# Exponentials and squares placed ahead of the cast of h's high part on ScalarE, in ticks that hold output products

## The chip, the cores and the metric

One core of a Trainium2 chip runs the whole program. The time is device time in microseconds (us) of one execution. The engines are TensorE (PE for its matmuls, PEld for its weight loads), VectorE (DVE), ScalarE (ACT), GpSimd (POOL) and SyncE (SP, which issues the DMAs). Each engine works through its own instructions in the order in which they stand.

## The reference

Windowed attention (8 batches, 8 heads, 576 positions, 64 wide; the first four heads look back 32 positions, the other four 128 positions in steps of 4), then RMS normalisation and a gated feed-forward, 512 to 1536 and back, over 4608 tokens:

```python
scores = np.where(masks[None], scale * np.matmul(q, k.transpose(0, 1, 3, 2)), -1e9)
attn = np.exp(scores - np.max(scores, axis=-1, keepdims=True))
attn = attn / (np.sum(attn, axis=-1, keepdims=True) + 1e-09)
x = np.matmul(attn, v).transpose(0, 2, 1, 3).reshape(B * S, H * D)
xn = x / np.sqrt(np.mean(x * x, axis=-1, keepdims=True) + 1e-06) * rms_g
g = xn @ w_gate
silu = g * (1.0 / (1.0 + np.exp(-g)))
return (silu * (xn @ w_val) @ w_out).astype(np.float32)
```

## The kernel before

The 4608 tokens are 16 units (u = 0 to 15) of 288. A unit's feed-forward runs over 12 blocks j of 128 hidden columns, and each block has three parts, called ticks here: gate (the product g, with `gate`), value (the product v, with `val`), and output, where `proj` multiplies h of the block before into four accumulators. A unit has so 36 ticks. From unit 1 on every operand x, w and h is split into a high part (rounded to the matmul's short format) and a low part (the rest), and each product is three matmuls: high by high, high by low, low by high (`three`, L652 and L655).

While the feed-forward of unit u runs, the attention of unit u + 1 is spread over its ticks: 14 bursts (a pair of heads c, a block i of queries) per unit. A burst has scores s (L508, L511), then the maximum on VectorE (`scores_max`, L384), exponentials on ScalarE (`scores_exp`, L395), the sum's reciprocal and a scaling on GpSimd (`scores_norm`, L411), transposes t of the weights on TensorE (L486), a copy pt of them out of PSUM on ScalarE with its low part on VectorE (`untranspose`, L466 and L468), output products o (L495 or L499), and their copy into xraw (`take` on ScalarE, L428 or L431; from unit 3 on `add` on VectorE, L441, for the low parts). When the last block of a pair of heads has been taken, `square` makes its squares for the norm (L447).

Nothing of this order is left to a scheduler: it is written out by hand. What follows a matmul group is put off with `later(dt, rank, fn)`: it is issued dt ticks later, and at the start of each tick `flush` issues what is due, smallest rank first, equal ranks as they came. Then the tick's matmuls are issued. In an output tick the ranks that bear on the change are: the product h = silu(g) * v on VectorE (`prod`, L710, rank 0), the copy pt (0.2), the casts of h's high part on ScalarE (`parts`, L721, 0.5) with its low part on GpSimd (L722), the copies by `take` (0.5), the exponentials (2), the squares (2.5), casts of k and q (3, 3.1) and of v's high part (3.3).

For PSUM two banks, "g" and "v", alternate between gate and value products: v of block j + 1 uses the bank that held g of block j. Where transposes fall into the output tick of block j, they are written into that same bank, so the value product of block j + 1 may not begin before ScalarE (L466) and VectorE (L468) have read them. This happens, for attention units from 3 on, after the blocks j = 1, 3, 5 and 11.

The tiles named in the profile: g, v and acc are the PSUM tiles of the three products, th the tanh and then h, hhi and hlo its parts, t the scores, weights or (on TensorE) the transposed weights, sum the row maxima and sums, pt the transposed weights in SBUF, sq the squares, xraw the attention's output.

Of the kernel before, what the change touches and what calls it, by code (L numbers as in the profile page):

```python
# [29 lines left out]
NEX = 3  # L30
# [31 lines left out]
def geometry(u, c):  # L62


    half = u % 2
    if c < NC // 2:
        if half:
            return [(QB * i, QB * i, 0, P) for i in range(U // QB)], QB, U + W
        return [(QB * i, max(QB * i - W, 0), 0 if i else W, P if i else QB)
                for i in range(U // QB)], QB, U  # L70
    nq = U // DIL
    keys = nq + (W if half else 0)
    return [(nq * r, keys * r, 0 if half else W, keys) for r in range(DIL)], nq, keys * DIL
# [3 lines left out]
def attn_moe(ctx: ExitStack, tc: tile.TileContext, qk_in, v_in, w_gate, w_val, w_out, rms_g, outT):  # L77
# [38 lines left out]
    now = [0]  # L116
    put_off = {}

    def later(dt, rank, fn):
        put_off.setdefault(now[0] + dt, []).append((rank, fn))  # L120
# [182 lines left out]
    def further(b, n):  # L303

        k = everything.index(b) + n
        return everything[k] if k < len(everything) else None
# [83 lines left out]
    def scores_exp(u, c, i):  # L390
        blocks, nq, _ = geometry(u, c)
        n = blocks[i][3]
        t, sm = st[u, c, i]
        for a in range(2):
            A.activation(out=t[:nq, a, :n], in_=t[:nq, a, :n], func=AF.Exp, scale=-1.0,  # L395
                         bias=sm[:nq, a, 0:1], accum_out=sm[:nq, a, 1:2] if u or i % 2 else None)
# [18 lines left out]
    def take(u, c, i, o):  # L415

        blocks, nq, _ = geometry(u, c)
        if (u, c) not in xraw:
            xraw[u, c] = sb.tile([P, U], F32, tag="xraw", name=f"xraw_{u}_{c}", bufs=NC)
        x = xraw[u, c]  # L420
        if c < NC // 2:
            to = x[:, QB * i:QB * i + nq]
        else:
            to = x.rearrange("p (j r) -> p r j", r=DIL)[:, i, :]
        copy = V.tensor_copy if i % 2 and u == 0 and c == NC - 1 else A.copy
        if u < NEX:
            for a in range(2):
                copy(out=to[a * D:(a + 1) * D], in_=o[a * D:(a + 1) * D, a * nq:(a + 1) * nq])  # L428
        else:
            for a in range(2):  # L430
                A.copy(out=to[a * D:(a + 1) * D], in_=o[a * D:(a + 1) * D, (2 + a) * nq:(3 + a) * nq])  # L431
        if i == len(blocks) - 1:
            later(1 if c != 1 or u < NEX else 4, 2.5 if u else 1.9, lambda: square(u, c))

    def add(u, c, i, o):
        _, nq, _ = geometry(u, c)
        x = xraw[u, c]
        to = x[:, QB * i:QB * i + nq] if c < NC // 2 else x.rearrange("p (j r) -> p r j", r=DIL)[:, i, :]
        for a in range(2):
            rows = slice(a * D, (a + 1) * D)  # L440
            V.tensor_tensor(out=to[rows], in0=o[rows, a * nq:(a + 1) * nq], in1=to[rows], op=ALU.add)  # L441

    def square(u, c):
        first = c == 0
        sq = sb.tile([P, U], F32, tag="xsq" if first else "tmp", name=f"sq_{u}_{c}", bufs=1 if first else 2)
        x = xraw[u, c]
        A.activation(out=sq, in_=x, func=AF.Square)  # L447
        if u == 0:
            G.tensor_scalar(out=x, in0=x, scalar1=gs[:, c:c + 1], scalar2=1.0, op0=ALU.mult, op1=ALU.mult)
        if first:  # L450
            xsq[u] = sq
        else:
            later(1, 0.4, lambda: (V if c == NC - 1 or u == 1 else G).tensor_tensor(out=xsq[u], in0=xsq[u], in1=sq, op=ALU.add))
# [6 lines left out]
    def untranspose(b, t_ps, wait):  # L460
        blocks, nq, _ = geometry(*b[:2])
        n = blocks[b[2]][3]
        t_in = t_ps[:n].rearrange("k (a q) -> k a q", a=2)[:, :, :nq]
        exact = b[0] < NEX
        st[b] = pt = sb.tile([P, 2, 2, QB], F32 if exact else F32R, tag="pt", name=f"pt_{b[0]}_{b[1]}_{b[2]}", bufs=2)
        A.copy(out=pt[:n, 0, :, :nq], in_=t_in)  # L466
        def low_part():
            V.tensor_tensor(out=pt[:n, 1, :, :nq], in0=t_in, in1=pt[:n, 0, :, :nq], op=ALU.subtract)  # L468

        if not exact:  # L470
            later(1, 0.4 if wait > 1 else -1.5, low_part) if wait else low_part()

    def products(q, t, o, t_ps, s_tag="s", o_tag="o", wait=0):


        if q:
            s_ps = ps.tile([P, 512], F32, tag=s_tag, name=f"s_{q[0]}_{q[1]}_{q[2]}")
        if o:
            o_ps = ps.tile([P, 512], F32, tag=o_tag, name=f"o_{o[0]}_{o[1]}_{o[2]}")
            pt = st.pop(o)  # L480
        if t:
            p, _ = st.pop(t)
        def transposed(a):
            blocks, nq, _ = geometry(*t[:2])
            n = blocks[t[2]][3]
            PE.transpose(t_ps[:n, a * QB:a * QB + nq], p[:nq, a, :n], ident[:nq, :nq])  # L486

        def output(a):
            blocks, nq, _ = geometry(*o[:2])
            n = blocks[o[2]][3]  # L490
            if a:
                return
            out = o_ps[:, :2 * nq].rearrange("d (a q) -> d a q", a=2)
            if o[0] < NEX:
                PE.matmul(out, vs.pop(o)[:n].rearrange("k a d -> k (a d)"), pt[:n, 0, :, :nq], start=True, stop=True)  # L495
                return
            vh, vl = (part[:n].rearrange("k a d -> k (a d)") for part in vparts[everything.index(o) % 2])
            both = o_ps[:, :4 * nq].rearrange("d (t a q) -> d t a q", t=2, a=2)
            PE.matmul(both, vh, pt[:n, :, :, :nq], start=True, stop=False)  # L499
            PE.matmul(out, vl, pt[:n, 0, :, :nq], start=False, stop=True)  # L500

        def scored(a):
            blocks, nq, _ = geometry(*q[:2])
            qc, kc, _, n = blocks[q[2]]
            sv = s_ps[:QB].rearrange("q (a t k) -> q a t k", a=2, t=2)
            if q[0] < NEX:
                qk = heads[q[0], 2 * q[1] + a]
                PE.matmul(sv[:nq, a, 0, :n], qk[:, qc:qc + nq], qk[:, U + kc:U + kc + n], start=True, stop=True)  # L508
                return
            qs, ks = heads[q[0], 2 * q[1] + a]  # L510
            PE.matmul(sv[:nq, a, :, :n], qs[:, qc:qc + nq], ks[:, :, kc:kc + n], start=True, stop=True)  # L511

        order = ((t, transposed), (o, output), (q, scored))
        if t and t[0] >= NEX:
            order = ((o, output), (t, transposed), (q, scored))
        parts = [(b, fn, a) for b, fn in order for a in range(2)]
        for b, fn, a in parts:
            if b:
                fn(a)
        if t:  # L520
            later(1, 0.2, lambda: untranspose(t, t_ps, wait))
        if o:
            later(1, 0.5, lambda: take(*o, o_ps))
            if o[0] >= NEX:
                later(2, -0.3, lambda: add(*o, o_ps))
            if o[0] < NEX:
                later(1, 9, lambda: load_v(further(o, 3)))
            far = further(o, 2)
            if far and far[0] >= NEX:
                split_v(far, 8 if o[0] < NEX else 1)  # L530
        if q:
            later(1, 0.7, lambda: scores_max(*q, s_ps))
            later(2, 2, lambda: scores_exp(*q))
            later(3 if q[0] < NNAT else 4, -1, lambda: scores_norm(*q))
            u, c, i = q
            nxt = after(u, 2 * c, 2)
            nb = len(geometry(u, c)[0])
            if u < NEX:
                if u == NNAT - 1 and c == NC - 1 and i == nb - 1:
                    for h in range(4):  # L540
                        later(1, 9, lambda h=h: load(NNAT, h))
                if u >= NNAT and i == nb - 1 and c < NC - 1:
                    for a in range(2):
                        later(1, 9, lambda a=a: load(*after(u, 2 * c + a, 4)))
                if u == NEX - 1 and c == NC - 1 and i == nb - 1:
                    for a in range(2):
                        later(3 + a, 9, lambda a=a: split(NEX, a, (1, 2, 2, 3), G, G))
            elif nxt and i == 0:
                split(*nxt, (1, 2, 2, 3), G, G)
                split(nxt[0], nxt[1] + 1, (2, 3, 3, 4) if c < NC - 1 else (1, 2, 3, 4), G, G)  # L550
# [245 lines left out]
    ends = nb + LAG + OUT + 5  # L796
# [127 lines left out]
```

## Time and profile before

| | |
|---|---|
| median of 3 runs | 1130.6 us (1130.0 to 1130.92) |
| the profiled execution | 1130.35 us |
| its span from first to last instruction | 1128.3 us |
| granted TensorE clock | 1.000 |
| idle time of ScalarE ahead of h's high part (L721) | 180.2 us, in 115 of 180 |

The page of the profile has, for 40 equal slices of the span, the busy share of each engine in tenths:

```profile
PE   8999999999999999999999999999999999999998
PEld 5787999999999999999999999999999999999998
ACT  6794676656576665657656575665657657575311
```

A timeline row reads: start in us, duration in us, engine, source line, operation, tile written <- tiles read, shapes, count; in brackets the idle time of the engine just before it and the instruction that ended it. A row of waits reads: who waited <- for whom, us in total, how often, the longest. Spans of matmuls overlap, so the distance from one start to the next tells more than the duration.

### The profile page before, as it was taken

To read this page: it belongs to the slowest core of one execution; us is meant where nothing else is said; L and a number is where in the kernel's file an instruction comes from. 1 tells how busy PE (TensorE), PEld (TensorE's weight loads), DVE (VectorE), ACT (ScalarE), POOL (GpSimd) and SP (SyncE) were. 2 spreads that over 40 slices of the span, in tenths; PEclk is the share of its full clock that TensorE was granted. 3 is DMA by queue.
4 is the path that set the end of the run, shared out by engine and by line. 5 is a ranking of instruction groups with operands and counts; after the bars stand their busy time and mean duration, and the time that the engine had idled before them with its cause. 6 is when DMAs were issued, how large, how long until landed. Compare 5 with 4: busy or idle time off the path is not lost.

```text
span 1128.3 us, 25465 instructions
## 1 busy us (share of the span) xinstructions
PE 1114.0 (99%) x8362; PEld 1078.7 (96%) x8362; DVE 672.4 (60%) x2734; ACT 701.5 (62%) x2579; POOL 674.9 (60%) x1154
## 2 busy tenths in 40 slices
PE   8999999999999999999999999999999999999998
PEld 5787999999999999999999999999999999999998
DVE  7889667556565565656556565665656556565412
ACT  6794676656576665657656575665657657575311
POOL 7423578656586665757657575675657656584311
PEclk9999999999999999999999999999999999999999
DMA  9664212212131131312212121130312212120000
GB/s 258 185 245 178 75 52 83 75 34 80 42 91 50 41 93 32 94 39 63 73 39 83 41 84 51 46 95 27 88 42 78 62 34 78 46 78 15 6 17 22
DMA packets 61542, 82.16 MB, mean 73 GB/s; under 512 B 7298, under 2 KB 41090, under 8 KB 61410
## 3 DMA queue, kind: packets, MB, share of 16 engines
q1 hardware_dynamic: 61410, 80.54, 23.9%
q8 instruction: 66, 1.08, 0.4%
q14 instruction: 66, 0.54, 0.2%
HBM read 71.08 MB, written 9.44 MB: 71 GB/s over the span
## 4 chain that ended last, share of the span: by engine, by line
PE 80%; ACT 7%; DVE 7%; POOL 2%; issue 2%; DMA 1%; SPq 0%; DVEq 0%; ACTq 0%; POOLq 0%
PE v L655 14%; PE acc L655 14%; PE g L655 14%; PE v L652 8%; PE acc L652 7%; PE g L652 7%; PE s L511 2%; PE acc L649 2%; PE o L499 2%; PE v L649 2%; ACT t L395 2%; PE g L649 2%; PE t L486 1%; ACT pt L466 1%; DVE pt L468 1%
## 5 line engine op out<-in xcount | busy, mean ns | idle before, releaser
L722 POOL TENSOR_TENSOR hlo<-th,hhi 128x288 fp32r<-128x288 f32 x179 | 145.8, 814 | 178.6 <-ACT hhi L721 165.9
L655 PE MATMUL acc<-hhi,lo 128*128 128x288 f32 x720 | 212.6, 295 | 0.0
L697 DVE SCALAR_TENSOR_TENSOR th<-th,g 128x288 f32<-128x288 f32 x180 | 81.8, 454 | 209.0 <-ACT pt L466 134.7
L721 ACT CAST hhi<-th 128x288 fp32r<-128x288 f32 x180 | 78.0, 433 | 180.2 <-DVE th L710 180.2
L655 PE MATMUL g<-xhi,lo 128*128 128x288 f32 x612 | 180.3, 295 | 0.0
L655 PE MATMUL v<-xhi,lo 128*128 128x288 f32 x612 | 180.1, 294 | 0.0
L411 POOL TENSOR_SCALAR t<-t,sum 72x72 f32<-72x72 f32 (+3 forms) x414 | 151.6, 378 | 35.5 <-DVE sum L405 23.2
L395 ACT ACTIVATE t<-t,sum 96x128 f32<-96x128 f32 (+3 forms) x448 | 165.1, 372 | 7.2 <-DVE sum L384 6.7
L323 POOL TENSOR_TENSOR vlo<-vt,vhi 128x128 fp32r<-128x128 f32 x182 | 84.2, 463 | 136.5 <-ACT vhi L319 134.5
L692 ACT ACTIVATE th<-g 128x288 f32<-128x288 f32 x180 | 73.9, 411 | 126.3 <-PE g L486 71.7
L655 PEld LDWEIGHTS acc<-hhi,lo 128*128 128x128 f32 x720 | 135.4, 188 | 0.0
L441 DVE TENSOR_TENSOR xraw<-o,xraw 64x72 f32<-64x72 f32 (+1 forms) x364 | 97.1, 267 | 39.2 <-ACT xraw L431 36.6
L655 PEld LDWEIGHTS g<-xhi,lo 128*128 128x128 f32 x612 | 115.2, 188 | 0.0
L655 PEld LDWEIGHTS v<-xhi,lo 128*128 128x128 f32 x612 | 115.0, 188 | 0.0
L652 PE MATMUL acc<-hhi,hi_o 128*128 128x288 f32 x360 | 109.1, 303 | 0.0
L652 PE MATMUL g<-xhi,hi_g 128*128 128x288 f32 x357 | 106.9, 299 | 0.0
L655 PE MATMUL acc<-hlo,hi_o 128*128 128x288 f32 x360 | 106.4, 296 | 0.0
L710 DVE TENSOR_TENSOR th<-th,v 128x288 f32<-128x288 f32 x180 | 81.0, 450 | 38.4 <-PE v L655 32.5
L431 ACT COPY xraw<-o 64x72 f32<-64x72 f32 (+1 forms) x364 | 95.3, 262 | 9.7 <-PE o L500 7.6
L353 POOL TENSOR_TENSOR ks<-qk,ks 128x288 fp32r<-128x288 f32 (+2 forms) x104 | 93.3, 902 | 3.1
L655 PE MATMUL g<-xlo,hi_g 128*128 128x288 f32 x322 | 95.1, 295 | 0.0
L362 POOL TENSOR_TENSOR qs<-qk,qs 64x288 fp32r<-64x288 f32 x104 | 84.1, 809 | 15.3 <-ACT qs L357 8.6
(188 smaller groups left out, 3528.7 us busy)
## 6 DMA issues: line engine op xcount, KB each, us to landing
qk<-in_qk_dram SPq DMA_DIRECT2D x60, 288.0 KB, 2.8
vt<-in_v_dram SPq DMA_DIRECT2D x196, 64.0 KB, 1.9
qk<-in_qk_dram SPq DMA_DIRECT2D x30, 352.0 KB, 3.0
out_dram<-ot SPq DMA_DIRECT2D x64, 144.0 KB, 1.9
qk<-in_qk_dram SPq DMA_DIRECT2D x30, 304.0 KB, 2.9
raw<-in_w_gate_dram SPq DMA_DIRECT2D x12, 512.0 KB, 6.0
raw<-in_w_val_dram SPq DMA_DIRECT2D x12, 512.0 KB, 5.3
raw<-in_w_out_dram SPq DMA_DIRECT2D x12, 512.0 KB, 4.1
```

What stands on the lines that cost most here:

```text
L323: G.tensor_tensor(out=vl, in0=vs.pop(b), in1=vh, op=ALU.subtract)
L353: ek.tensor_tensor(out=ks[:, 1, :nkt], in0=kr, in1=ks[:, 0, :nkt], op=ALU.subtract)
L362: eq.tensor_tensor(out=qs[D:], in0=qr[D:], in1=qs[D:], op=ALU.subtract)
L395: A.activation(out=t[:nq, a, :n], in_=t[:nq, a, :n], func=AF.Exp, scale=-1.0, bias=sm[:nq, a, 0:1], accum_out=sm[:nq, a, 1:2] if u or i % ...
L411: (V if u == 0 and (c, i) > (NC - 1, 0) else G).tensor_scalar(out=t[:nq, a, :n], in0=t[:nq, a, :n], scalar1=sm[:nq, a, 3:4], scalar2=1.0, ...
L431: A.copy(out=to[a * D:(a + 1) * D], in_=o[a * D:(a + 1) * D, (2 + a) * nq:(3 + a) * nq])
L441: V.tensor_tensor(out=to[rows], in0=o[rows, a * nq:(a + 1) * nq], in1=to[rows], op=ALU.add)
L652: PE.matmul(out, wh[:, cc, :], xh, start=start, stop=False)
L655: PE.matmul(out, w[:, cc, :], v, start=False, stop=stop and k == 1)
L697: V.scalar_tensor_tensor(out=t, in0=t, scalar=1.0, in1=g, op0=ALU.add, op1=ALU.mult)
L710: V.tensor_tensor(out=t, in0=t, in1=v_ps[:, :U], op=ALU.mult)
L722: (V if (u, j) == (NU - 1, NJ - 1) else G).tensor_tensor(out=lo, in0=t, in1=hi, op=ALU.subtract)
```

## The change

Two ranks change. The exponentials of a burst whose scores were issued in a gate tick (`wait == 1`) come two ticks later, in an output tick; they get rank 0.42 in place of 2, and so stand behind pt (0.2) and ahead of h's high part (0.5) and of `take`. The squares of units from 3 on get 0.44 where they fall into an output tick.

```diff
         if i == len(blocks) - 1:
-            later(1 if c != 1 or u < NEX else 4, 2.5 if u else 1.9, lambda: square(u, c))
+            dt = 1 if c != 1 or u < NEX else 4
+            later(dt, 0.44 if u >= NEX and (now[0] + dt - ends) % 3 == 0 else 2.5 if u else 1.9, lambda: square(u, c))
...
             later(1, 0.7, lambda: scores_max(*q, s_ps))
-            later(2, 2, lambda: scores_exp(*q))
+            later(2, 0.42 if wait == 1 else 2, lambda: scores_exp(*q))
```

No instruction is added or removed, and only ScalarE's instructions change places: 77 pairs of exponentials and 26 squares. The diff lengthens the file by one line, so lines from 434 on have numbers one higher after it.

The first place is ScalarE's order in the output tick of block j = 1 in the feed-forward of unit 5, before the change (`hhi_1` and `th_1` are those of block 1; `t_2_1` is a burst of attention unit 6, `sq_0` its first squares, `pt_1_2` the copy that the next value product's bank waits for):

```order
L319 CAST vhi_2277<-vt_1_1_5446 128x128
L721 CAST hhi_1_5926<-th_1_5884 128x288
L395 ACTIVATE t_2_1_5891,sum_87<-t_2_1_5891,sum_87 72x72 x2
L447 ACTIVATE sq_0_5935<-xraw_0_5749 128x288
L466 CAST pt_1_2_5962<-t_1_5953 128x192
```

The same place in the changed kernel:

```order
L319 CAST vhi_2277<-vt_1_1_5446 128x128
L395 ACTIVATE t_2_1_5891,sum_87<-t_2_1_5891,sum_87 72x72 x2
L448 ACTIVATE sq_0_5928<-xraw_0_5749 128x288
L722 CAST hhi_1_5930<-th_1_5884 128x288
L467 CAST pt_1_2_5962<-t_1_5953 128x192
```

The two exponentials and the square now stand ahead of the cast, and the copy pt directly behind it.

The second place is the output ticks of blocks 3 and 4 of the same feed-forward and the two ticks between, on ScalarE, before:

```order
L721 CAST hhi_3_6121<-th_3_6081 128x288
L395 ACTIVATE t_3_0_6088,sum_90<-t_3_0_6088,sum_90 72x72 x2
L357 CAST qs_0_6127<-qk_0_5896 128x288
L466 CAST pt_2_2_6152<-t_3_6143 72x2x72
L431 COPY xraw_2_6155<-o_2_0_6145 64x72 x2
L357 CAST qs_1_6165<-qk_1_5931 128x288
L319 CAST vhi_2277<-vt_2_2_5974 128x128
L692 ACTIVATE th_4_6190<-g_4_6171 128x288
L395 ACTIVATE t_3_1_6158,sum_86<-t_3_1_6158,sum_86 72x72 x2
L466 CAST pt_2_3_6221<-t_4_6211 72x2x72
L721 CAST hhi_4_6223<-th_4_6190 128x288
L431 COPY xraw_2_6155<-o_2_1_6213 64x72 x2
```

And in the changed kernel:

```order
L395 ACTIVATE t_3_0_6088,sum_90<-t_3_0_6088,sum_90 72x72 x2
L722 CAST hhi_3_6123<-th_3_6081 128x288
L357 CAST qs_0_6127<-qk_0_5896 128x288
L467 CAST pt_2_2_6152<-t_3_6143 72x2x72
L431 COPY xraw_2_6155<-o_2_0_6145 64x72 x2
L357 CAST qs_1_6165<-qk_1_5935 128x288
L319 CAST vhi_2277<-vt_2_2_5974 128x128
L693 ACTIVATE th_4_6190<-g_4_6171 128x288
L395 ACTIVATE t_3_1_6158,sum_86<-t_3_1_6158,sum_86 72x72 x2
L467 CAST pt_2_3_6221<-t_4_6211 72x2x72
L448 ACTIVATE sq_1_6223<-xraw_1_5965 128x288
L722 CAST hhi_4_6225<-th_4_6190 128x288
```

After block 3 the exponentials of `t_3_0` have gone ahead of the cast; those of `t_3_1`, whose scores came in another tick, stay where they were. After block 4 the square `sq_1`, which stood behind the output copies (L431), has gone ahead of the cast and of these copies.

## The prediction

> **What bounds the kernel now.** I read the page first, then the waits grouped by who waited for whom, then the timeline around one such wait, engine by engine.
>
> ```profile
> span 1128.3 us, 25465 instructions
> PE 1114.0 (99%) x8362; PEld 1078.7 (96%) x8362; DVE 672.4 (60%) x2734; ACT 701.5 (62%) x2579; POOL 674.9 (60%) x1154
> ```
>
> TensorE is the bound: its matmul row leaves 1128.3 - 1114.0 = 14.3 us free, its weight-load row 1128.3 - 1078.7 = 49.6 us. ScalarE is free for more than a third of the span. So a shorter ScalarE alone buys nothing; only a wait of TensorE that ends with ScalarE's work can.
>
> The Trainium skill, "Perfetto Trace Analysis", section "Identifying the Most-Contended Engine", says that the busy share of matmuls misleads because they are pipelined, and that the busy share of weight loads is the better measure of room. By its first number a gain over 14.3 us would be excluded, by its second only one over 49.6 us. The trace agrees as far as the next rows go: it shows waits in front of weight loads that the matmul row, whose entries overlap, hardly shows, and it lowers the chance of the first rival below.
>
> The waits of the weight loads, and those of matmuls, VectorE and ScalarE that bear on it (total us, times, longest us):
>
> ```profile
> PEld v L652 <- DVE pt L468: 8.2, 26, 0.5
> PEld v L652 <- DVE sum L404: 1.5, 7, 0.2
> PEld o L499 <- issue: 1.1, 4, 0.4
> PEld o L495 <- ACT xraw L428: 0.8, 2, 0.6
> PE v L652 <- DVE pt L468: 1.4, 7, 0.2
> DVE pt L468 <- ACT pt L466: 72.6, 52, 1.9
> ACT hhi L721 <- DVE th L710: 180.2, 115, 2.3
> ```
>
> The largest wait of TensorE is at the start of a value product: v may not write its PSUM bank before VectorE (L468) has read the transposed weights out of the same bank, and VectorE waits for ScalarE's copy of them (L466). ScalarE, in turn, sits idle 180.2 us in front of h's high part. The second row is the same place: L404 stands right behind L468 on VectorE and ends when the wait does.
>
> How one such opening looks, in the feed-forward of unit 5 after block j = 1, and how one looks after j = 7, where no transposes share the bank:
>
> ```profile
> 405.30 0.19 PEld L655 LDWEIGHTS g<-spare,lo 128*128 128x128 f32 x1
> 405.77 0.19 PEld L652 LDWEIGHTS v<-xhi,hi_o 128*128 128x128 f32 x1 [0.28 <-DVE pt L468]
> 405.88 0.19 PEld L655 LDWEIGHTS v<-xlo,hi_o 128*128 128x128 f32 x1
> 406.01 0.19 PEld L655 LDWEIGHTS v<-xhi,lo 128*128 128x128 f32 x1
> ```
>
> ```profile
> 438.60 0.19 PEld L655 LDWEIGHTS g<-spare,lo 128*128 128x128 f32 x1
> 438.74 0.19 PEld L652 LDWEIGHTS v<-xhi,hi_v 128*128 128x128 f32 x1
> 438.87 0.19 PEld L655 LDWEIGHTS v<-xlo,hi_v 128*128 128x128 f32 x1
> 439.01 0.19 PEld L655 LDWEIGHTS v<-xhi,lo 128*128 128x128 f32 x1
> ```
>
> From g's last load to v's third: 406.01 - 405.30 = 0.71 us against 439.01 - 438.60 = 0.41 us. The difference, 0.30 us, is the 0.28 us of the row: such a wait is lost by TensorE in full.
>
> **The change part by part.** It adds and removes no instruction. Only ScalarE's order changes: 77 pairs of exponentials and 26 squares go one or two places forward. 65 of the pairs (five for each of the units 3 to 15, after j = 1, 3, 5, 9 and 11) and all the squares go in front of h's high part. After j = 1, 3 and 5 the transposed weights share v's bank (after j = 11 too, but there v opens without a wait); in the feed-forwards of units 2 to 14 that makes 13 x 3 = 39 places, and the three rows of v above count 26 + 7 + 7 = 40 waits, 8.2 + 1.5 + 1.4 = 11.1 us.
>
> ScalarE, VectorE and TensorE in the 4 us ahead of the opening after j = 1:
>
> ```profile
> 403.53 0.43 ACT L721 CAST hhi<-th 128x288 fp32r<-128x288 f32 x1 [1.63 <-DVE th L710]
> 403.86 0.35 ACT L395 ACTIVATE t<-t,sum 72x72 f32<-72x72 f32 x1
> ...
> 404.56 0.43 ACT L447 ACTIVATE sq<-xraw 128x288 f32<-128x288 f32 x1
> 405.01 0.32 ACT L466 CAST pt<-t 128x192 fp32r<-128x192 f32 x1
> ```
>
> ```profile
> 401.97 0.08 DVE L384 DVE_READ_ACCUMULATOR2_ANT sum<- 72x1 f32 x1
> ...
> 402.50 0.51 DVE L441 TENSOR_TENSOR xraw<-o,xraw 64x96 f32<-64x96 f32 x2
> 403.04 0.46 DVE L710 TENSOR_TENSOR th<-th,v 128x288 f32<-128x288 f32 x1
> 405.36 0.36 DVE L468 TENSOR_TENSOR pt<-t,pt 128x192 fp32r<-128x192 f32 x1 [1.87 <-ACT pt L466]
> ```
>
> ```profile
> 403.62 0.33 PE L486 MATMUL t<-ident,t 96*128 96x96 f32 x2
> ...
> 403.92 0.34 PE L652 MATMUL g<-xhi,hi_o 128*128 128x288 f32 x1
> ```
>
> Step 1, does the moved work fit into the idle 1.63 us? The exponentials need the maxima, done at 401.97 + 0.08 = 402.05. They take 404.56 - 403.86 = 0.70 us, so they end near 402.8. The square needs VectorE's additions into xraw, done at 402.50 + 0.51 = 403.01, and takes 405.01 - 404.56 = 0.45 us: until about 403.5. The product that h's high part waits for ends at 403.04 + 0.46 = 403.50. So h's high part still begins near 403.53, at worst 0.1 us later.
>
> Step 2, what then comes sooner? Behind h's high part stands the copy pt directly. It began at 405.01; now it begins when ScalarE is through with the high part (403.86) and the transposes are out (403.62 + 0.33 = 403.95), so near 404.0: 1.0 us sooner. VectorE has been idle for 1.87 us, so L468 moves with it, to about 404.4 to 404.7. The bank is free 0.7 us before v's first load would like it (405.30 + 0.14 = 405.44). The wait after j = 1 is gone, for any size up to the longest, 0.5 us.
>
> Step 3, the other two places. After j = 3 a q cast stays in front of pt, and after j = 5 nothing does:
>
> ```profile
> 413.54 0.08 DVE L384 DVE_READ_ACCUMULATOR2_ANT sum<- 72x1 f32 x1
> 415.04 0.43 ACT L721 CAST hhi<-th 128x288 fp32r<-128x288 f32 x1 [1.19 <-DVE th L710]
> 416.51 0.27 ACT L466 CAST pt<-t 72x144 fp32r<-72x144 f32 x1
> ```
>
> ```profile
> 424.85 0.08 DVE L384 DVE_READ_ACCUMULATOR2_ANT sum<- 72x1 f32 x1
> 426.41 0.43 ACT L721 CAST hhi<-th 128x288 fp32r<-128x288 f32 x1 [1.87 <-DVE th L710]
> 427.55 0.27 ACT L466 CAST pt<-t 72x144 fp32r<-72x144 f32 x1
> ```
>
> The maxima are ready 415.04 - 413.62 = 1.42 and 426.41 - 424.93 = 1.48 us ahead of the high part, ScalarE is idle for 1.19 and 1.87 us, and the pair takes 0.70 us, so it fits at both places; pt and L468 come about 0.7 us sooner, more than the longest wait. I take all three terms in full: -11.1 us.
>
> Step 4, what is pushed back. After j = 9 the maxima are late:
>
> ```profile
> 446.27 0.08 DVE L384 DVE_READ_ACCUMULATOR2_ANT sum<- 96x1 f32 x1
> 447.00 0.43 ACT L721 CAST hhi<-th 128x288 fp32r<-128x288 f32 x1 [1.69 <-DVE th L710]
> 448.59 0.46 POOL L573 TENSOR_TENSOR rst_lo<-rst,rst_hi 96x3 fp32r<-96x3 f32 x1
> 449.01 0.82 POOL L722 TENSOR_TENSOR hlo<-th,hhi 128x288 fp32r<-128x288 f32 x1
> ```
>
> There the exponentials begin at 446.35 and, being wider, take some 0.8 us, so the high part starts 0.15 to 0.3 us later. Its reader on GpSimd, the low part, starts at 449.01 behind the root's low part anyway, 1.6 us after the high part ends: hidden. After j = 4 a square alone goes in front of high part and output copies, where ScalarE does not idle: both come about 0.4 us later. What covers it is the distance to the next reader on TensorE. Here for j = 1, where the high part ended at 403.96:
>
> ```profile
> 404.04 0.80 POOL L722 TENSOR_TENSOR hlo<-th,hhi 128x288 fp32r<-128x288 f32 x1 [0.74 <-ACT hhi L721]
> 407.98 0.34 PE L652 MATMUL acc<-hhi,hi_o 128*128 128x288 f32 x1
> ```
>
> The low part ends at 404.84, 3.1 us before the output products want it. If that cover were gone, 13 squares of 0.45 us would cost up to 6 us. I take 0. The other 12 pairs belong to units 1 and 2, in an earlier stage where no v waits for pt; 5 of them go in front of output copies (L428). The nearest row is that of output products waiting for those copies, 0.8 us in two waits: these may go, or as much may come again, -0.8 to +0.8 us; I take 0.
>
> The sum goes against the profiled execution's own 1130.35 us (span 1128.3 and 2.05 around it; 0.25 below the median of the runs, 1130.6): 1130.35 - 11.1 = **1119.2 us**.
>
> **The rivals.**
>
> - **The waits reappear elsewhere on TensorE.** If the next thing is late by the same amount (the product L710 read out before g reuses the bank, or VectorE's additions before the next output product), nothing is won: 1130.3 us. For it: a 99% busy matmul row. Against it: L710 ends at 403.50 and the next g opens at 403.92, and both hang on TensorE's own progress, so they move together. In between, **half is won**: the waits after j = 3 and 5 or the longer ones after j = 1 remain in part, 1130.35 - 5.5 = 1124.8 us. Against it: pt comes 0.7 to 1.0 us sooner at all three, and no wait is longer than 0.5 us.
> - **Slower: ScalarE held by late maxima.** Exponentials that wait for VectorE block the high part, pt and tanh behind them. It decides where the maxima end less than 0.7 us ahead of the high part's start, as after j = 9 (0.65 us). If its 0.2 us reached TensorE once in each of 13 units, 2.6 us: 1133.0 us. Against it: GpSimd's 449.01 above and the 3.1 us. The Trainium skill, "Perfetto Trace Analysis", section "Tensor Engine Instruction (MATMUL, LD_WEIGHTS)", calls ScalarE's queue strictly first in, first out; it speaks for this rival wherever an input is late. The trace agrees: at 402.05 the exponentials' input was there, and ScalarE idled until 403.53 because the high part stood ahead of them.
> - **It does not take effect.** If the moved exponentials still ended after the product, pt would come as late as before: 1130.3 us. Against it: 1.4 us between maxima and high part at the three places.
>
> **How the numbers follow.** Forecast 1119.2 us with its own range of 1117.3 (the output products' 1.1 and 0.8 us of waits go too) to 1121.5 (a fifth of the term stays): chance 0.78. Half won: 0.12, faster as well. Nothing won, by the first or third rival: 0.06. Slower: 0.04. The range must reach to the half case to leave out no more than 2 in 10: 1117.3 to 1124.8. A measurement of this kernel can tell about 0.2% (2.3 us) from no change; so faster 0.90, within it 0.06, slower 0.04.
>
> **What would show it.** Right: the three rows of v waiting for L468 or L404 vanish or fall under 1 us; idle time before the high part falls from 180.2 us by some 65 x 0.7 plus 13 x 0.4, to about 130; VectorE's wait for pt falls from 72.6 us by 30 us or more; the weight loads' busy sum stays at 1078.7 us in a span of about 1117. Wrong: a new row of TensorE waiting for L710, L441 or GpSimd of several us; or the v rows still there, with exponentials that idle in front of the high part; or a matmul spacing other than 0.13 us, which nothing here would explain.

## The result and the profile after

The changed kernel takes 1116.87 us (median of 4 runs, 1116.29 to 1121.66) beside 1130.76 us (median of 4, 1130.0 to 1131.88): a ratio of 0.9886, 95% interval 0.9857 to 0.9914. The profiled executions are 1116.57 and 1130.35 us, 13.8 us apart, where 11.1 us were forecast. The median lies 0.4 us below the low end of the range, and 2.3 us below the predicted time. The execution of 1121.66 us had a mean granted clock of 0.995, the other three 1.000.

The page of the changed kernel, and the weight loads' waits of over 0.4 us that are not of the first 45 us:

```profile
span 1114.8 us, 25463 instructions
PE 1102.5 (99%) x8362; PEld 1076.9 (97%) x8362; DVE 670.9 (60%) x2734; ACT 708.8 (64%) x2579; POOL 674.7 (61%) x1154
```

```profile
PEld bps L602 <- ACT rd L586: 0.8, 2, 0.6
...
PEld o L500 <- issue: 0.5, 2, 0.3
```

All rows of v waiting for L468 (now L469) or L404 are gone. One wait of v is left in this and every other run, 2.0 us in unit 0 (L650, before L649, for pt); where a run below is said to have no waiting v, it is units 1 to 15 that are meant. The same 8362 matmuls have 11.5 us less busy time: before, the matmuls that waited in TensorE were booked as busy. The weight loads' sum hardly moved (1078.7 to 1076.9 us). So the share of matmuls, 99% both times, could not have shown what was to be had. The rule of the Trainium skill ("Perfetto Trace Analysis", "Identifying the Most-Contended Engine") says so too, of pipelined matmuls in general; what hid the room here was waiting booked as busy time.

The waits on ScalarE and VectorE that the change moves:

```profile
ACT hhi L722 <- DVE th L711: 84.7, 88, 1.9
...
ACT t L395 <- DVE sum L384: 32.0, 51, 4.0
...
DVE pt L469 <- ACT pt L467: 35.8, 39, 1.1
```

Idle time ahead of h's high part fell from 180.2 to 84.7 us. A part of it now stands ahead of the exponentials, 32.0 us where it was 6.7 before, because they get to the front before the maxima are there. VectorE's wait for pt fell from 72.6 to 35.8 us.

The engines' shares of the chain that ended last, before and after:

```profile
PE 80%; ACT 7%; DVE 7%; POOL 2%; issue 2%; DMA 1%; SPq 0%; DVEq 0%; ACTq 0%; POOLq 0%
```

```profile
PE 94%; POOL 2%; ACT 1%; DVE 1%; DMA 1%; issue 1%; SPq 0%; POOLq 0%; ACTq 0%; DVEq 0%
```

Before, the chain left TensorE again and again for ScalarE and VectorE, 14% of it together; now 2%.

The same opening as in the prediction, after block 1 of unit 5's feed-forward. ScalarE, then VectorE, then the weight loads:

```profile
398.21 0.36 ACT L395 ACTIVATE t<-t,sum 72x72 f32<-72x72 f32 x1
...
398.57 0.34 ACT L395 ACTIVATE t<-t,sum 72x72 f32<-72x72 f32 x1
398.81 0.19 ACT L395 ACTIVATION_READ_ACCUMULATOR t<-t,sum 72x1 f32 x1
399.32 0.45 ACT L448 ACTIVATE sq<-xraw 128x288 f32<-128x288 f32 x1 [0.32 <-DVE xraw L442]
399.81 0.43 ACT L722 CAST hhi<-th 128x288 fp32r<-128x288 f32 x1
400.27 0.32 ACT L467 CAST pt<-t 128x192 fp32r<-128x192 f32 x1
```

```profile
399.32 0.45 DVE L711 TENSOR_TENSOR th<-th,v 128x288 f32<-128x288 f32 x1
400.62 0.36 DVE L469 TENSOR_TENSOR pt<-t,pt 128x192 fp32r<-128x192 f32 x1 [0.85 <-ACT pt L467]
```

```profile
401.57 0.19 PEld L656 LDWEIGHTS g<-spare,lo 128*128 128x128 f32 x1
401.70 0.19 PEld L653 LDWEIGHTS v<-xhi,hi_o 128*128 128x128 f32 x1
401.84 0.19 PEld L656 LDWEIGHTS v<-xlo,hi_o 128*128 128x128 f32 x1
401.98 0.19 PEld L656 LDWEIGHTS v<-xhi,lo 128*128 128x128 f32 x1
```

Exponentials and square fill what was idle; the high part starts 0.04 us after its product ends (399.32 + 0.45 = 399.77), as before; pt stands 0.46 us behind it instead of 1.48. From g's last load to v's third: 0.41 us, the undisturbed figure.

### The profile page after: what moved, and what is told of

It is laid out like the page before. It is cut to its first block, busy times and chain, and to the rows that moved or that the text cites. A ratio compares the mean times of both kernels' runs of the same rounds, so it can differ in the third digit from the quotient of the medians.

```text
span 1114.8 us, 25463 instructions
## 1 busy us (share of the span) xinstructions
PE 1102.5 (99%) x8362; PEld 1076.9 (97%) x8362; DVE 670.9 (60%) x2734; ACT 708.8 (64%) x2579; POOL 674.7 (61%) x1154
## 4 chain that ended last, share of the span: by engine, by line
PE 94%; POOL 2%; ACT 1%; DVE 1%; DMA 1%; issue 1%; SPq 0%; POOLq 0%; ACTq 0%; DVEq 0%
PE acc L656 17%; PE g L656 17%; PE v L656 17%; PE acc L653 9%; PE g L653 8%; PE v L653 8%; PE s L512 3%; PE o L500 3%; PE acc L650 2%; PE v L650 2%; PE g L650 2%; PE t L487 2%; PE o L501 1%; PE g L487 1%; PE o L496 1%; PE s L509 1%
## 5 line engine op out<-in xcount | busy, mean ns | idle before, releaser
L698 DVE SCALAR_TENSOR_TENSOR th<-th,g 128x288 f32<-128x288 f32 x180 | 81.8, 454 | 213.0 <-ACT pt L467 124.7
L656 PE MATMUL v<-xhi,lo 128*128 128x288 f32 x612 | 180.2, 294 | 0.0
L722 ACT CAST hhi<-th 128x288 fp32r<-128x288 f32 x180 | 77.8, 432 | 85.3 <-DVE th L711 84.7
L711 DVE TENSOR_TENSOR th<-th,v 128x288 f32<-128x288 f32 x180 | 81.0, 450 | 54.7 <-PE v L656 53.0
L431 ACT COPY xraw<-o 64x72 f32<-64x72 f32 (+1 forms) x364 | 95.5, 262 | 9.7 <-PE o L501 7.6
```

Of the source, the lines that this page charges most:

```text
L656: PE.matmul(out, w[:, cc, :], v, start=False, stop=stop and k == 1)
L698: V.scalar_tensor_tensor(out=t, in0=t, scalar=1.0, in1=g, op0=ALU.add, op1=ALU.mult)
L711: V.tensor_tensor(out=t, in0=t, in1=v_ps[:, :U], op=ALU.mult)
```

## The experiments

All started from the changed kernel; line numbers are as in it, one higher behind an added line. The theory: TensorE lost time only where v waits for its bank until ScalarE has copied pt, so what counts is ScalarE's time in front of pt. The rivals: the early exponentials help by themselves, through the scaling and the transposes; the squares are needed; or the places after j = 4, 9 and 11 do a part.

| run | us, median | its runs | ratio to before, 95% interval |
|---|---|---|---|
| exponentials alone | 1118.03 | 1116.03 to 1120.31 | 0.9899 (0.9879 to 0.992) |
| squares alone | 1126.9 | 1126.02 to 1130.62 | 0.9976 (0.9963 to 0.9988) |
| after j = 1, 3, 5 only | 1118.69 | 1118.0 to 1121.69 | 0.9904 (0.9889 to 0.9919) |
| everywhere else | 1129.56 | 1128.7 to 1133.2 | 0.9995 (0.9985 to 1.0006) |
| two more casts after j = 3 | 1125.62 | 1124.86 to 1126.26 | 0.9953 (0.9938 to 0.9968) |
| exponentials behind pt | 1120.53 | 1120.16 to 1123.56 | 0.9914 (0.9898 to 0.993) |
| exponentials a tick earlier | 1117.67 | 1117.41 to 1118.19 | 0.9884 (0.9867 to 0.99) |
| one more cast after j = 3 | 1118.15 | 1117.67 to 1121.69 | 0.9891 (0.9867 to 0.9915) |

The kernel before, measured along with them, had medians of 1130.67 (first four), 1130.78 (next three) and 1131.82 us (last).

**Exponentials alone.**

```diff
-            later(dt, 0.44 if u >= NEX and (now[0] + dt - ends) % 3 == 0 else 2.5 if u else 1.9, lambda: square(u, c))
+            later(dt, 2.5 if u else 1.9, lambda: square(u, c))
```

> The squares go back to rank 2.5, the exponentials stay ahead of h's high part. Theory (v waits for its bank until pt is copied, and only ScalarE's time in front of pt counts): after j = 1 pt still comes about 0.7 us sooner, more than the longest wait of 0.5 us, so nothing of the gain is lost: 1116.5 to 1117.5 us. Rival (the squares carry their part of the gain after j = 1, 0.45 of 1.15 us moved): about 2 of the 5.3 us there come back, near 1119 us.

Two executions took 1116.0 us and two 1120 us; the profiled one, 1116.05 us, is as fast as the changed kernel, and no v waits in it. From unit 2 on its trace is 13.4 us shorter than that of before, as much as the changed kernel's. The squares are not needed. The rival falls.

**Squares alone.**

```diff
-            later(2, 0.42 if wait == 1 else 2, lambda: scores_exp(*q))
+            later(2, 2, lambda: scores_exp(*q))
```

> The exponentials go back to rank 2, the squares stay at 0.44. Theory: after j = 1 pt comes 0.45 us sooner, which removes nearly all of that place's 5.3 us; after j = 3 and 5 (3.7 and 2.5 us) nothing changes: 1125 to 1126 us. Rival (it is the early exponentials, through the reciprocal, the scaling and the transposes, that help): no gain, 1130.6 us.

3.8 us of gain. Weight loads of v still wait:

```profile
PEld v L653 <- DVE pt L469: 3.3, 13, 0.4
...
PEld v L653 <- DVE sum L404: 1.6, 7, 0.2
```

13 waits in place of 26 in the first row. The loss at an opening can also be read from the matmuls' own starts: the distance from the matmul ahead of v to v's third, less the 0.4 us of an undisturbed opening. Added up over the units, this loss is 0.9 us after j = 1 (5.3 before), 3.6 after j = 3 (3.7) and 2.6 after j = 5 (2.5). So the squares alone cure most of the first place, and each place answers to what stands in front of its own pt. The gain came out some 1 us under the expectation, mostly by what is left after j = 1.

**The three places, and all the others.** The first of these runs keeps the moved ranks only after j = 1, 3 and 5; the second only elsewhere (`not` in front of the bracketed condition, 14 in place of 5).

```diff
-            later(2, 0.42 if wait == 1 else 2, lambda: scores_exp(*q))
+            later(2, 0.42 if q[0] >= NEX and (now[0] + 4 - ends) % 36 in (5, 11, 17) else 2, lambda: scores_exp(*q))
...
-            later(dt, 0.44 if u >= NEX and (now[0] + dt - ends) % 3 == 0 else 2.5 if u else 1.9, lambda: square(u, c))
+            later(dt, 0.44 if u >= NEX and (now[0] + dt + 2 - ends) % 36 == 5 else 2.5 if u else 1.9, lambda: square(u, c))
```

> Only the exponentials and squares after j = 1, 3 and 5 of units 2 to 14 move (39 pairs, 13 squares); the other 38 pairs and 13 squares stay as before the change. Theory: the whole of the value products' wait goes, 11.4 us, with the small waits of the same units; only what units 0 and 1 gained (0.7 us by the traces) stays away: 1117 to 1118.5 us. Rival (the places after j = 9 and 11 and after j = 4 do part of it): 1120 us or more.

> The complement: the 38 pairs and 13 squares that the run with three places leaves out move, and those after j = 1, 3 and 5 stay as before the change. Theory: the value products wait as before, only the 0.7 us of units 0 and 1 go: 1129.5 to 1130.5 us, the three rows of v at 11 us. Rival (those places do part of it): 1125 to 1128 us; rival (squares and exponentials ahead of high part and output copies cost something where ScalarE has no idle time): over 1131 us.

Three places: 1118.69 us, and no v waits. Its profiled execution is behind the changed kernel by 0.7 us in units 0 and 1 and by one wait of 1.0 us of an output product in unit 4's feed-forward. Everywhere else: no difference that this measurement can tell (interval 0.9985 to 1.0006), and v waits as before the change:

```profile
PEld v L653 <- DVE pt L469: 8.4, 27, 0.5
...
PEld v L653 <- DVE sum L404: 1.4, 6, 0.2
```

So most of the gain sits at the three places. The other 38 pairs and 13 squares cost nothing that shows; in the trace they gain 0.7 us in units 0 and 1 and 0.6 us after that, most of it at two output products o after j = 1, which together is less than this measurement can tell.

**Two more casts, then one, after j = 3.** The values are written twice (once) more, so only time is added.

```diff
-            A.copy(out=hi, in_=t)
+            for _ in range(3 if j == 3 else 1):
+                A.copy(out=hi, in_=t)
```

> The changed kernel, with h's high part cast three times over instead of once after j = 3 alone (the same values twice more; 0.33 us of ScalarE each, between the early exponentials and pt). Theory (ScalarE's time between the transposes and pt is what counts): pt comes 0.67 us later, nearly as late as before the change, and v waits 3.2 to 3.7 us in all after j = 3, nowhere else: 3 to 4 us over the changed kernel, 1119.5 to 1121 us. Rival (the exponentials' early results are what helps): they are as early as in the changed kernel, so 1116 to 1117.5 us.

Some 5 us more than expected. ScalarE after block 3 of unit 5's feed-forward, and the waits of weight loads and matmuls of v:

```profile
413.82 1.36 ACT L723 CAST hhi<-th 128x288 fp32r<-128x288 f32 x3 [0.49 <-DVE th L711]
415.09 0.43 ACT L357 CAST qs<-qk 128x288 fp32r<-128x288 f32 x1
415.54 0.27 ACT L467 CAST pt<-t 72x144 fp32r<-72x144 f32 x1
```

```profile
PEld v L653 <- DVE pt L469: 6.1, 13, 0.6
...
PE v L653 <- DVE pt L469: 3.1, 12, 0.3
```

Three casts took 1.36 us and one takes 0.43, so a repeat into the same tile cost 0.46 us, not the 0.33 us from one ScalarE instruction to the next that I had worked with. pt came 415.54 - 413.82 = 1.72 us behind the high part's start, 0.25 us later than before the change (416.51 - 415.04 = 1.47); the odd units' loss of 0.23 to 0.24 us at this place became 0.48, just that much more. In all, 6.5 us were lost at v's openings after j = 3, where 3.2 to 3.7 were expected, and 1.2 us more at the transposes behind v of block 4, of which the part on the prediction below has more. Places after j = 1 and 5 stayed free. The early exponentials, kept in this run, did not save it: that rival falls. With the measured 0.46 us the next run was predicted:

> As the run with three casts after j = 3, but with two. There a cast that repeats took 0.46 us, not 0.33, so pt came 0.25 us later than before the change and v waited 0.5 to 0.7 us at each place. Theory: with one repeat pt is 0.46 us later than in the changed kernel, which is 0.2 us sooner than before the change; of the 0.39 us that an even unit's v waited before, about 0.15 us come back (7 places), of the 0.24 us of an odd unit's at most 0.05 us: 1 to 1.5 us in all, 1117.5 to 1118.5 us. Rival (a share that goes with the casts' time, without a threshold): half of the 8.7 us that two repeats cost, 1121 us.

1118.15 us. At v's openings after j = 3, added up over starts of matmuls, 0.08 to 0.13 us were lost in even units and 0.02 to 0.03 in odd ones, 0.7 us in all. No, one and two repeats cost 0, 0.7 and 6.5 us there: a threshold, not a share. The median came out as expected, but the theory's term was not all of it: a further 1.0 us was lost at the transposes behind v of block 4.

**Exponentials behind pt.**

```diff
-            later(2, 0.42 if wait == 1 else 2, lambda: scores_exp(*q))
+            later(3 if wait == 1 and q[0] >= NNAT else 2, 2, lambda: scores_exp(*q))
```

> The same pairs of exponentials of units 2 to 15 are put off by a tick, behind pt and the output copies, in place of being drawn ahead of h's high part; the squares as in the changed kernel. Theory: pt is again directly behind the high part, so v waits nowhere after j = 1, 3 and 5; the later exponentials feed transposes 4 ticks on: 1116.5 to 1119 us. Rival (early exponentials help): slower than before the change, over 1131 us. A second way to miss: VectorE's sums, first in line in the value tick, wait for the late exponentials and hold the product for h: some us of the gain come back.

1120.53 us, and no v waits. Here the exponentials are later than they were before the change, and still 10 us are won: what helps is the empty road in front of pt. The second way to miss, named ahead, came true in part. VectorE's sums wait for the late exponentials, and transposes for VectorE's th (L698):

```profile
DVE sum L404 <- ACT t L395: 30.9, 46, 1.0
PEld t L487 <- DVE th L698: 1.1, 6, 0.2
```

L698 is silu, so it is silu that comes late and not, as expected, the product for h. By the starts of the matmuls the run is 3.8 us behind the changed kernel: 2.0 us of it at the transposes behind v of block 4, and 1.7 us in unit 1, where the weight loads of scores wait 1.6 us for the maxima (L384); the changed kernel has 0.4 us of such waits.

**Exponentials a tick earlier.**

```diff
-            later(2, 0.42 if wait == 1 else 2, lambda: scores_exp(*q))
+            later(1 if wait == 1 else 2, 0.75 if wait == 1 else 2, lambda: scores_exp(*q))
```

> The same pairs of exponentials are issued a tick earlier still, in the value tick, behind tanh, pt and the output copies and in front of the casts of k, q and v's high part, where VectorE's maxima are not yet done. Theory: ScalarE idles in front of the exponentials until the maxima come and the casts start 0.7 us later; the high part is 0 to 0.4 us late; pt is as early as in the changed kernel after j = 1 and 5 and about 0.3 us sooner than before the change after j = 3, where up to 1.5 us of wait remain: 1116.5 to 1119 us. Rival (late maxima hold ScalarE's whole queue and TensorE feels it): over 1120 us.

1117.67 us, within what the measurement can tell of the changed kernel, and no v waits. ScalarE idles ahead of the exponentials twice as long as in the changed kernel:

```profile
ACT t L395 <- DVE sum L384: 66.1, 81, 3.7
```

So strict order with late inputs does hold ScalarE, for 66.1 us in all, but it has slack for that, and TensorE does not feel it. The slower rival falls as to its price, not as to its mechanism.

## Why the prediction was right, and where it was off

- **The bound and the step that frees it: right, and shown.** v's rows are gone, and the run everywhere else leaves them untouched. The term of 11.1 us was sized well: by the starts of the matmuls, the loss at v's openings fell from 11.4 to 0.1 us.
- **Step 1 (the moved work fits) held**, with a detail that I had wrong: the pair does not wait for both maxima. Each exponential waits for its own: in unit 5 after j = 9 the first starts at 441.82, and the second maximum ends at 441.91 + 0.08 = 441.99. So here, where I put the high part 0.15 to 0.3 us later, it was not late at all; its product (L711) ended at 442.18 + 0.43 = 442.61:

```profile
441.82 0.40 ACT L395 ACTIVATE t<-t,sum 96x128 f32<-96x128 f32 x1 [0.86 <-DVE sum L384]
442.12 0.18 ACT L395 ACTIVATION_READ_ACCUMULATOR t<-t,sum 96x1 f32 x1
442.22 0.39 ACT L395 ACTIVATE t<-t,sum 96x128 f32<-96x128 f32 x1
442.51 0.18 ACT L395 ACTIVATION_READ_ACCUMULATOR t<-t,sum 96x1 f32 x1
442.64 0.43 ACT L722 CAST hhi<-th 128x288 fp32r<-128x288 f32 x1
```

- **Step 2 held**: I put pt near 404.0, 0.5 us behind the high part's start; it is 0.46 behind, and the high part was not late. L469 ends at 400.62 + 0.36 = 400.98, 0.7 us ahead of v's first load (401.70), as I had it.
- **Step 4's zeros held** to within what can be measured (the run everywhere else).
- **One of the signs was off**: idle time ahead of the high part was to fall to about 130 us and fell to 84.7. I counted the moved work alone; idle time also moved, ahead of the exponentials (from 6.7 to 32.0 us) and of others. The other signs came as said: v's rows gone, VectorE's wait for pt down by 36.8 us, the weight loads' sum within 2 us.
- **What was mis-sized is the sum's remainder.** I let only two rows of small waits, 1.9 us, bound what else could go, and took 0. From TensorE's first matmul into acc (unit 0) to the end the changed kernel gains 14.1 us (it began that matmul 0.56 us later), of which 11.3 us at v's openings, 0.7 us in units 0 and 1 and some 2 us elsewhere. The largest part of the last has no row among the waits. In even units the transposes behind v of block 4 were held up by VectorE's silu (L697), which reads the bank they share:

```profile
351.70 0.23 PE L500 MATMUL o<-pt,vlo 104*128 104x144 f32 x1
351.88 0.33 PE L486 MATMUL t<-ident,t 72*104 72x72 f32 x2
```

```profile
349.51 0.31 DVE L468 TENSOR_TENSOR pt<-t,pt 104x144 fp32r<-104x144 f32 x1 [1.87 <-ACT pt L466]
...
351.38 0.45 DVE L697 SCALAR_TENSOR_TENSOR th<-th,g 128x288 f32<-128x288 f32 x1
```

```profile
348.38 0.23 PE L501 MATMUL o<-pt,vlo 104*128 104x144 f32 x1
348.44 0.29 PE L487 MATMUL t<-ident,t 72*104 72x72 f32 x2
```

```profile
345.83 0.31 DVE L469 TENSOR_TENSOR pt<-t,pt 104x144 fp32r<-104x144 f32 x1 [1.14 <-ACT pt L467]
...
347.70 0.46 DVE L698 SCALAR_TENSOR_TENSOR th<-th,g 128x288 f32<-128x288 f32 x1
```

  Unit 4's feed-forward, before (first two) and after (last two). The transposes followed the output product o by 0.18 us and now by 0.06. silu ended at 351.83, just ahead of the transposes' start. It did not wait for ScalarE's tanh, which had ended at 350.63 + 0.41 = 351.04; it is late for the same reason as v: it starts 1.87 us behind pt's low part in both kernels (351.38 - 349.51, 347.70 - 345.83), with VectorE's other work between them, and that low part waits for ScalarE's copy. So a copy that comes sooner brings silu forward too. From v's last matmul to acc's third behind it, each of the 7 even units gains 0.15 to 0.18 us, and all units together 1.2 us. The runs bear it out: the exponentials alone win the 1.2 us, the run everywhere else does not, and with one and two casts more after j = 3 they are 1.0 and 1.2 us behind the changed kernel at this place. Two output products o after j = 1 (units 4 and 10) make another 0.7 us; these the run everywhere else wins as well, and the row of output products fell from 1.1 to 0.5 us. Some 0.3 us stay, in pieces of 0.05 us and less, which I leave open.
- **The rivals.** Nothing and half won did not come: no wait on TensorE took the place of the one removed, and the exponentials did take effect ahead of the product. That was argued from one opening; the three-place run shows it for all 39. Late maxima did hold ScalarE, but TensorE did not feel it (the run a tick earlier).

## What to carry to other kernels

On an engine that looks 99% busy, look for waits at the openings of its accumulation groups and compare one that waits with one that doesn't, start to start: the difference times the count is what a fix is worth. Then ask what stands in front of the releasing instruction on its own engine; work that is ready while that engine idles belongs ahead of the idle time, and here it helped whether that work got earlier or later, though later cost some 4 us elsewhere. Look too at what stands behind the released instruction on the next engine: silu, behind pt's low part, was late with it. Beyond the point at which the wait ends, more slack buys nothing here.

## What the runs showed of the hardware that was not expected

A cast of 128x288 repeated into the same tile started 0.46 us behind the one before, 0.03 us after its end, while the q cast behind the three of them started 0.09 us before the third one's end (413.82 + 1.36 = 415.18 against 415.09). The trace's records of these instructions show a difference: each repeat waits for the semaphore that ScalarE itself raises after the cast ahead, and the q cast does not. So what was lost is the overlap of two instructions, to a wait that the program carries. A different tile does not ensure the overlap either: pt, which waits for TensorE's semaphore, started 0.45 us behind the q cast (415.54 - 415.09), though the transposes that it reads had ended at 414.22. What decides there was not tried.

The granted TensorE clock can drop early in an execution though matmuls fill most of the time. In the profiled execution of the run everywhere else the windows of 10 us from 20 to 40 us show clocks of 0.90 and 0.75, with TensorE busy 8.82 and 9.68 of 10 us:

```profile
20.00:30.00 10.00, 8.82 (x50) 6.10 (x50) 8.49 (x38) 7.53 (x32) 5.89 (x9) 0.90 1.04 249
30.00:40.00 10.00, 9.68 (x44) 7.79 (x43) 4.73 (x19) 4.95 (x16) 6.48 (x10) 0.75 0.88 164
```

The columns are the window, its length, busy time and instructions of TensorE's matmuls, its weight loads, VectorE, ScalarE and GpSimd, then the clock, the DMA share and GB/s. In the profiled execution of before the same windows had clock 1.00 and 56 matmuls each, not 50 and 44. The longest time without a matmul between 20 and 40 us is 0.43 us in both executions, so a pause of TensorE there does not tell them apart. What set the drop off was not tried.
